# Batch 3's softmax denominators from a sum made on GpSimd, and an earlier place for one group of batch 2's query transpositions

## The chip, the cores and the metric

The kernel runs on one core of a Trainium2 chip. The metric is the device time of one execution in microseconds; the time before is the median of three runs, 233.81 us (233.22 to 233.97).

## The reference

The computation is an attention over 32 memory slots followed by a gated feed-forward layer. For each of 8 batches and 8 heads, with 576 positions and head width 64:

```python
a = softmax(phi, axis=positions)                  # 576 x 32, normalized over the positions
k_m = einsum('bhsm,bhsd->bhmd', a, k)             # 32 x 64
v_m = einsum('bhsm,bhsd->bhmd', a, v)
attn = softmax(q @ k_m^T / sqrt(64), axis=slots)  # 576 x 32
x = attn @ v_m                                    # heads side by side: 4608 x 512
out = (silu(x @ w_gate) * (x @ w_val)) @ w_out    # 512 -> 1536 -> 512
```

The first softmax needs, for each head and slot, a denominator: the sum of exp(phi) over the 576 positions. It is applied to the two sums over positions, k_m and v_m, once they are there.

## The kernel before

**Tiling.** Work goes batch by batch. Positions lie nine to a partition (JK = 9), and a head takes 64 partitions, so two heads (NG = 2 groups) fill the 128 partitions and there are four pairs of them. v_m is multiplied into w_gate and w_val first (`u_round`, L460), which gives the matrices t_U; the attention weights t_A are then the moving operand of the gate and value products (`gv_half`, L515). ScalarE takes silu of the gate (L532), VectorE multiplies it with the value (L538) into t_h. One batch has 24 such gate and value slots. The output product t_h times w_out is a two by two block product with seven instead of eight block products: its operands are sums and differences of blocks, t_S of t_h (L603 and L560, on GpSimd or VectorE) and t_T of w_out (`weight_sums`, L562, on VectorE).

**Output products.** `products` (L689) returns them as 42 small units in a fixed order: `first` (units 0 to 5 into bank p_os, 6 to 11 into p_oa), `five` (12 to 17, bank p_oc), `six` (18 to 23, p_os again), `three` (24 to 29, p_oc again), `seven` and `four`. A unit is two matrix products of 128x256 (L727), one for each half of 256 positions. Units 0 and 1 of a product use chunk 0 of the hidden width, 2 and 3 chunk 1, 4 and 5 chunk 2. After a product's last unit a copy on ScalarE (`keep`, L752, tiles t_p and t_q) or an add on VectorE (L757) reads the bank, and a bank used again waits for that.

**Order.** The order on every engine is the order in which the code is written out (L62). Items of a batch are Python closures, run by hand in lists (`run`) or put among each other by a numeric place (`spread`). An engine does its own instructions in order; where one needs a result of another engine it waits, and what stands behind it on that engine waits too. TensorE's weight loads (LDWEIGHTS) go ahead of the product that is running.

**Banks.** The eight PSUM banks are handed out from a list, the longest free first (`bank`, `done`, L75 to L84). A bank's next user waits for the last reader of the user before.

**Batch 2's start (L999 to L1024).** TensorE runs batch 0's remaining output products and, among them, batch 2's attention: k and v sums over positions (`kv_sum`, L222, tiles p_kv, one bank for each group), their normalization on VectorE (`kv_norm`, L268, four operations at L266 into t_bkv), their transposition on TensorE (`kv_T`, L278: three products at L288 into p_T, copied to t_kT by VectorE, L289), and the transposition of the queries in three groups of six (`q_T`, L377: products at L383 into p_q, copied to t_qT by ScalarE, L337). Then the scores follow (`scores`, L392: products at L396, exponentials at L407). VectorE makes the weight differences t_T meanwhile (L560). A copy of one element on GpSimd, `wait_for` (L642, tile t_mark, L645), holds GpSimd until a given tile is there; here it waits for the last of the t_T. After it GpSimd makes eight block sums of batch 1 and issues batch 4's four loads (`loads`, q, phi, k, v; L108, L94, L99, L103).

**Denominators (`kv_denominators`, L239).** exp(phi) lies in t_ephi as nine tiles of 128x128 (a position in nine, times four head pairs with 32 slots). Without further work TensorE multiplies each of the nine with `ones2`, 128x2, and adds them up in PSUM: nine weight loads and nine products two columns wide (L258). Where a batch is in `esums`, GpSimd has added the nine tiles first (`phi_sum`, L205: a mark that waits for the batch before's t_A, four adds at L212, a cast to bfloat16 at L218 and the remainder at L219), and TensorE has two products, with the sum's high and low part (tile t_ehl). Before the change batches 4, 6 and 7 are in `esums`; 2, 3 and 5 are not.

**`kv_items` (L292).** For a batch in `esums` the denominators come behind the k and v sums and a further round of products (`behind`), in a p_kv bank. For one that is not, they come first, in a bank of their own, p_S (`own`). The k and v sums of batch b + 1 are put at place 6 of the 24 slots of batch b.

Of the kernel before, what the change touches and what calls it, by code (L numbers as in the profile page):

```python
# [14 lines left out]
def kernel(  # L15
# [59 lines left out]
    def bank(shape, dtype, name):  # L75
        tag = free.pop(0)
        t = ps.tile(shape, dtype, tag=tag, name=name)
        held[id(t)] = tag, t
        return t

    def done(*tiles):

        for t in tiles:
            free.append(held.pop(id(t))[0])  # L84
# [29 lines left out]
    def load_qT(b):  # L114

        qTs[b] = att.tile([128, NS, 128], BF16, tag="qT", name="t_qT")
        nc.sync.dma_start_transpose(out=qTs[b], in_=qs[b])
# [52 lines left out]
    def phi_exp(b):  # L170
        t = att.tile([128, JK, NP, M], BF16, tag="ephi", name="t_ephi")
        nc.scalar.activation(
            out=t.rearrange("p j i m -> p i j m"),
            in_=phis.pop(b).rearrange("p i (j m) -> p i j m", m=M),
            func=AF.Exp,
        )
        ephis[b] = t
# [25 lines left out]
    esums = {}  # L203
# [18 lines left out]
    def kv_sum(b, p, parts):  # L222


        w0, w1 = parts[0], parts[-1] + 1
        n = (w1 - w0) * D
        for j in range(JK):
            for i in range(NP):
                for g in range(NG):
                    nc.tensor.matmul(  # L230
                        p[g][32 * i:32 * i + 32, 0:n],
                        lhsT=phi_of(b, g, j, i),
                        rhs=kvs[b][64 * g:64 * g + 64, w0:w1, i, j * D:(j + 1) * D],
                        start=(j == 0),
                        stop=(j == JK - 1),
                        tile_position=(64 * g, 32 * i),
                    )

    def kv_denominators(b, p):  # L239

        if b in masked:
            for g in range(NG):
                for j in range(JK):
                    nc.tensor.matmul(
                        p[:, g:g + 1],
                        lhsT=masked[b][:, j, g].rearrange("p i m -> p (i m)"),
                        rhs=ones1,
                        start=(j == 0),
                        stop=(j == JK - 1),
                    )  # L250
            return
        if b in esums:
            hl = esums.pop(b)
            terms = [hl[:, t] for t in range(2)]
        else:
            terms = [ephis[b][:, j].rearrange("p i m -> p (i m)") for j in range(JK)]
        for n, x in enumerate(terms):
            nc.tensor.matmul(p, lhsT=x, rhs=ones2, start=(n == 0), stop=(n == len(terms) - 1))  # L258

    def kv_reciprocal(b, p):  # L260
        r = att.tile([128, NG], FP32, tag="rS", name="t_rS")
        nc.vector.reciprocal(out=r, in_=p)
        rSs[b] = r
# [4 lines left out]
    def kv_norm(b, p):  # L268

        t = att.tile([128, 3, 128], BF16, tag="bkv", name="t_bkv")  # L270
        for g in range(NG):
            x = p[g][:, 0:D].rearrange("p (a d) -> p a d", a=1).to_broadcast([128, 2, D])
            scaled_copy(t[:, g].rearrange("p (a d) -> p a d", a=2), x, rSs[b][:, g:g + 1])
            scaled_copy(t[:, 2, D * g:D * g + D], p[g][:, D:2 * D], rSs[b][:, g:g + 1])
            done(p[g])
        bkvs[b] = t

    def kv_T(b):  # L278


        kTs[b] = att.tile([128, 3, 128], BF16, tag="kT", name="t_kT")
        t = bkvs.pop(b)
        if b > 3:
            nc.sync.dma_start_transpose(out=kTs[b], in_=t.rearrange("p n x -> p (n x)"))
            return
        p = bank([128, 3, 128], BF16, "p_T")
        for n in (2, 0, 1):
            nc.tensor.transpose(p[:, n], t[:, n], ident)  # L288
        nc.vector.tensor_copy(out=kTs[b], in_=p)  # L289
        done(p)  # L290

    def kv_items(b, beside=None):  # L292


        def run_sums():
            o = 2 * D
            behind = b in esums
            own = beside and not behind
            if own:
                d = bank([128, NG], FP32, "p_S")  # L300
                kv_denominators(b, d)
                kv_reciprocal(b, d)
                done(d)
            p = [bank([128, CH], FP32, f"p_kv{g}") for g in range(NG)]
            if not (own or behind):
                kv_denominators(b, p[0][:, o:o + NG])
            kv_sum(b, p, (0, 1))
            if behind:
                beside()
                kv_denominators(b, p[0][:, o:o + NG])  # L310
            if not own:
                kv_reciprocal(b, p[0][:, o:o + NG])
            kv_norm(b, p)
            if beside and not behind:
                beside()

        return [run_sums, lambda: kv_T(b)]
# [530 lines left out]
    def run(items):  # L848
        for x in items:
            x()  # L850
# [10 lines left out]
    def exp_tables():  # L861
        nc.scalar.preload_act_table_set("natural_log_exp_and_others")
# [127 lines left out]
    def run_late():  # L990
        run(late)
        late.clear()
# [3 lines left out]
    for b in range(2, B):  # L996
        last = b + 1 == B
        exp_tables()
        if b == 2:  # L999
            load_qT(3)  # L1000
            phi_exp(2)
            (zero, ops0), (one, ops1) = products(0, ("c11",)), products(1, ("p1", "c11"))
            kv, q2 = kv_items(2), q_items(2, "aaa")
            run(zero[:6])
            sums = {n: f for n, f in zip(((1, 1), (0, 2), (1, 2)), late)}
            late.clear()
            sums[0, 2]()
            weight_sums(0)
            weight_sums(1)
            run(zero[6:12] + one[:6] + kv[:1] + q2[:2])  # L1010
            weight_sums(2, (0, 1))
            run(zero[12:16] + zero[18:22] + kv[1:] + q2[2:] + zero[16:18] + zero[22:24])
            weight_sums(2, (2, 3))
            ops0["c11"]()
            ops1["p1"]()
            wait_for(Ts[2][0:1, 3, 0, 0:1])
            for part in ((0, 1), (3,), (2,)):
                for c in (1, 2):
                    sums[1, c](part)
            loads(4)  # L1020
            backlog = one[6:12] + zero[36:] + one[12:36]
            ops = ops1
        else:
            run(take(6))  # L1024
        for g in range(NG):
            scores(b, g)
        if b > 2:
            ops["p1"]()
            u_values(b)
        else:  # L1030
            run(zero[24:36] + take(6))
        run(take(6))
        z_inv_v(b, 0)
        ops["c11"]()
        run(take(6))
        if not last:
            phi_exp(b + 1)
        z_inv_v(b, 1)
        if b > 2:
            norm(b, 0)  # L1040
            norm(b, 1)
        run(take(6))
        run_late()
        if b == 4:
            wait_for(atts[4, 1][0:1, 0, 0:1])
            quad_sums(0)
        nc.scalar.preload_act_table_set("silu_and_others")
        run(take(6))
        if b == 2:
            norm(2, 0)  # L1050
        run(take(6))
        if b == 2:
            norm(2, 1)
            u_three(2)
            run(one[36:])
        g = gv_slots(b)
        quad = []
        if b == 4:
            quad = products(b, (), 0)[0]
        if last:  # L1060
            rest, rest_ops = products(b, (), 1)
            backlog += rest[:12]
        beside = 0 if last else 2 if quad else min(4, len(backlog))
        outs = [lambda: run(take(1)) for _ in range(len(backlog) - beside)]
        streams = [(g, 0, 24), (quad[:12], 0, 3), (quad[12:], 12, 18.5)]
        streams += [(outs, 4, 7 if quad else 24)]
        if b == 2:
            streams += [([lambda: u_values(2)], 2.5, 3)]
        if last:
            streams += [([u_item(b, 2)], 5, 6)]  # L1070
        if not last:
            if b > 2:
                load_qT(b + 1)
            if b > 2 and b != 4:
                phi_sum(b + 1)
            streams += [
                (kv_items(b + 1, lambda: (u_item(b, 2, "aava")(), run(take(2)))), KV, KV + 4),
                ([lambda: (u_three(b + 1), run(take(2)))], 19, 20),
            ]
        spread(*streams)  # L1080
        flush_mul()
        units, ops = products(b, ("p1", "c11"))
        backlog += units
# [34 lines left out]
```

## Time and profile before

| | |
|---|---|
| median of three runs | 233.81 us (233.22 to 233.97) |
| profiled execution, span from first to last instruction | 231.4 us; its time with what lies around the span is not listed |
| median less span | 2.4 us |
| TensorE busy | 221.6 us, 96% |
| VectorE, ScalarE, GpSimd busy | 185.1, 171.7, 140.8 us |
| batch 2's transpositions and scores | 59.1 to 63.6 us |
| batch 3's denominators, p_S | at 79.98 us |

In the profile PE is TensorE's products, PEld its weight loads, DVE VectorE, ACT ScalarE, POOL GpSimd, SP SyncE. A line of a timeline has the start in us from the span's start, the duration of what is merged in it, the engine, the line in the code, the operation, the tile written and those read, the shape and the count; in brackets stands the idle time before it and what ended it. Products are pipelined: each lasts longer than the step from one to the next. The ends of products are modelled.

### The profile page before, as it was taken

The page shows a single profiled execution, that of the slowest core. Times are in us where ns is not written, and L with a number is a line of the kernel's source. Part 1 is how long each engine was busy: PE and PEld are TensorE (multiplying, and loading weights), DVE is VectorE, ACT ScalarE, POOL GpSimd, SP SyncE. Part 2 cuts the span into 40 slices and gives each one's busy share as a digit, 9 for nine tenths or more (in the row PEclk, how much of TensorE's full clock was granted, in tenths as well). Part 3 has the DMA queues.
Part 4 walks back from the last instruction along what each step waited for, and adds up shares of the span by engine and source line. Part 5 has one row for each costly group of instructions (what it writes and reads, how often), then busy time and mean ns, then how long its engine had stood idle before and what let it go on. Part 6 is the DMA issues. An engine that isn't in the chain of part 4 may idle for free.

```text
span 231.4 us, 7210 instructions
## 1 busy us (share of the span) xinstructions
PE 221.6 (96%) x2825; PEld 169.8 (73%) x2825; DVE 185.1 (80%) x423; ACT 171.7 (74%) x365; POOL 140.8 (61%) x190
## 2 busy tenths in 40 slices
PE   6987799999999999999999999999999999999993
PEld 2544476778887777878788787887788778878882
DVE  4245789999966799989997668998999899977732
ACT  2777898988447989968896658978898789677310
POOL 8422427998199049765977689464845394039291
PEclk9999999999999999999999999999999999999998
DMA  6999999999996992999299946994014502202125
GB/s 214 210 211 206 199 207 207 221 245 268 205 225 175 256 256 49 223 204 184 71 223 191 226 134 115 252 236 89 28 65 114 104 0 95 91 10 84 31 85 160
DMA packets 36674, 36.84 MB, mean 159 GB/s; under 512 B 14624, under 2 KB 31008, under 8 KB 36640
## 3 DMA queue, kind: packets, MB, share of 16 engines
q0 software_dynamic: 16272, 22.42, 52.5%
q1 hardware_dynamic: 19600, 13.18, 22.9%
q10 hardware_dynamic: 768, 0.79, 1.1%
q8 instruction: 22, 0.36, 0.6%
q14 instruction: 12, 0.10, 0.1%
HBM read 42.47 MB, written 9.44 MB: 224 GB/s over the span
## 4 chain that ended last, share of the span: by engine, by line
PE 86%; DMA 9%; POOL 2%; ACT 1%; issue 0%; DVE 0%; POOLq 0%
PE p_g L515 21%; PE p_os L727 21%; PE p_v L515 20%; PE p_oc L727 10%; DMA W<-in_moe_w_val_dram 9%; PE p_oa L727 5%; PE p_u L472 5%; PE p_kv L230 2%; PE p_g L396 1%; POOL t_kv L99 1%; POOL t_kv L103 1%; PE p_q L383 0%; POOL t_q L108 0%; ACT t_qT L337 0%; POOL W L138 0%
## 5 line engine op out<-in xcount | busy, mean ns | idle before, releaser
L538 DVE TENSOR_TENSOR t_h<-t_sg,p_v 128x288 bf16<-128x288 bf16 x192 | 81.8, 451 | 14.1 <-PE p_v L515 7.0
L515 PEld LDWEIGHTS <-t_U 128*128 128x128 bf16 x768 | 73.9, 98 | 21.2 <-issue 3.5
L532 ACT ACTIVATE t_sg<-p_g 128x288 bf16<-128x288 f32 x192 | 73.3, 424 | 17.1 <-PE p_g L515 11.4
L515 PE MATMUL p_g<-t_A,t_U 128*128 128x288 bf16 x384 | 77.0, 286 | 0.0
L515 PE MATMUL p_v<-t_A,t_U 128*128 128x288 bf16 x384 | 77.0, 286 | 0.0
L727 PEld LDWEIGHTS <-t_S 128*128 128x128 bf16 x384 | 37.5, 98 | 4.5 <-issue 0.2
L603 POOL TENSOR_TENSOR t_S<-t_h 128x512 bf16<-128x512 bf16 x17 | 19.7, 1157 | 32.7 <-DVE t_h L538 31.2
L727 PEld LDWEIGHTS <-t_h 128*128 128x128 bf16 x288 | 27.1, 98 | 8.6 <-issue 5.0
L492 ACT CAST t_U<-p_u 128x512 bf16<-128x512 f32 x51 | 27.0, 605 | 6.6 <-PE p_u L472 6.6
L727 PE MATMUL p_os<-t_T,t_S 128*128 128x256 bf16 x192 | 23.7, 273 | 0.0
L560 POOL TENSOR_TENSOR t_S<-t_S,t_h 128x512 bf16<-128x512 bf16 x17 | 19.6, 1156 | 1.3
L560 POOL TENSOR_TENSOR t_S<-t_h 128x512 bf16<-128x512 bf16 x16 | 18.4, 1152 | 0.0
L560 POOL TENSOR_TENSOR t_S<-t_h,t_S 128x512 bf16<-128x512 bf16 x16 | 18.4, 1152 | 0.0
L472 PE MATMUL p_u<-W,t_kT 64*32 64x512 bf16 (+1 forms) x416 | 15.3, 363 | 1.2 <-DMA W<-in_moe_w_gate_dram 0.6
L496 DVE CAST t_U<-p_u 128x512 bf16<-128x512 f32 x21 | 13.6, 683 | 1.9 <-PE p_u L472 1.9
L727 PE MATMUL p_os<-t_T,t_h 128*128 128x256 bf16 x96 | 14.8, 273 | 0.0
L875 PE MATMUL p_warm<-bones 128*128 128x512 bf16 x44 | 12.5, 421 | 1.7 <-DVE bones L897 1.7
L452 DVE TENSOR_TENSOR t_A<-t_E,t_lz 128x576 bf16<-128x576 bf16 x16 | 11.4, 740 | 0.7 <-ACT t_lz L428 0.7
L727 PE MATMUL p_oc<-t_T,t_S 128*128 128x256 bf16 x96 | 11.9, 273 | 0.0
L727 PE MATMUL p_oa<-WO,t_h 128*128 128x256 bf16 x96 | 11.8, 273 | 0.0
L727 PE MATMUL p_oc<-WO,t_S 128*128 128x256 bf16 x96 | 11.8, 272 | 0.1
L727 PE MATMUL p_os<-WO,t_h 128*128 128x256 bf16 x96 | 11.8, 273 | 0.0
(107 smaller groups left out, 308.3 us busy)
## 6 DMA issues: line engine op xcount, KB each, us to landing
out_dram<-t_o SPq DMA_DIRECT2D x11, 512.0 KB, 3.0
t_kv<-in_k_dram POOLq DMA_DIRECT2D x8, 576.0 KB, 10.5
t_q<-in_q_dram POOLq DMA_DIRECT2D x8, 576.0 KB, 8.4
t_kv<-in_v_dram POOLq DMA_DIRECT2D x8, 576.0 KB, 14.7
t_phi<-in_phi_dram POOLq DMA_DIRECT2D x6, 576.0 KB, 8.1
out_dram<-t_o SPq DMA_DIRECT2D x10, 256.0 KB, 4.5
WO<-in_moe_w_out_dram POOLq DMA_DIRECT2D x3, 512.0 KB, 19.2
W<-in_moe_w_gate_dram POOLq DMA_DIRECT2D x2, 512.0 KB, 16.5
```

The lines of the kernel that those rows point to most:

```text
L230: nc.tensor.matmul(p[g][32 * i:32 * i + 32, 0:n], lhsT=phi_of(b, g, j, i), rhs=kvs[b][64 * g:64 * g + 64, w0:w1, i, j * D:(j + 1) * D], st ...
L452: nc.vector.tensor_tensor(out=a, in0=es.pop((b, g)), in1=lzs.pop((b, g)), op=ALU.mult)
L472: nc.tensor.matmul(p[g][32 * i:32 * i + 32, o:o + n], lhsT=kTs[b][64 * g:64 * g + 64, 2, 32 * i:32 * i + 32], rhs=w_part(w, c, i, g, halve ...
L492: nc.scalar.copy(out=t, in_=p)
L496: nc.vector.tensor_copy(out=t, in_=p)
L515: nc.tensor.matmul(p[:, 0:HALF], lhsT=Us[b, c, g][:, o // 2, which, 128 * (o % 2):128 * (o % 2 + 1)], rhs=atts[b, g][:, r], start=(g == 0) ...
L532: nc.scalar.activation(out=sg, in_=gate[:, 0:HALF], func=AF.Silu)
L538: nc.vector.tensor_tensor(out=dst, in0=sg, in1=val[:, 0:HALF], op=ALU.mult)
L560: eng.tensor_tensor(out=out, in0=x, in1=y, op=ALU.subtract)
L603: eng.tensor_tensor(out=t[:, 0], in0=A21, in1=A22, op=ALU.add)
L727: nc.tensor.matmul(mine[home][:, u], lhsT=lhs(c, m, u), rhs=rhs(c, m), start=fresh and u == 0, stop=(k == 5), skip_group_check=u == 1 or n ...
L875: nc.tensor.matmul(p[:, 0:128 * a], lhsT=bones, rhs=x.to_broadcast([128, a, 128]) if a > 1 else bones, start=True, stop=True,)
```

## The change

Three lines change. The first two belong together: batch 3's exponentials are summed by GpSimd as well (`phi_sum(3)` is called in batch 2's main stretch, ahead of its slots), and its denominators stay ahead of the k and v sums in a bank of their own, now as two products instead of nine. The third moves the third group of batch 2's query transpositions ahead of the first eight products of `six` and of the transposition of t_bkv.

```diff
         def run_sums():
             o = 2 * D
-            behind = b in esums
+            behind = b in esums and b != 3
             own = beside and not behind
...
             weight_sums(2, (0, 1))
-            run(zero[12:16] + zero[18:22] + kv[1:] + q2[2:] + zero[16:18] + zero[22:24])
+            run(zero[12:16] + q2[2:] + zero[18:22] + kv[1:] + zero[16:18] + zero[22:24])
             weight_sums(2, (2, 3))
...
             if b > 2:
                 load_qT(b + 1)
-            if b > 2 and b != 4:
+            if b != 4:
                 phi_sum(b + 1)
```

On GpSimd seven instructions come in between batch 4's loads and batch 2's first block sum: the mark, four adds, a cast and a subtraction. On TensorE seven weight loads and seven products go, six products with their loads move, and the banks of p_T and p_q are exchanged. VectorE and ScalarE keep their instructions and their order.

## Prediction

> **What bounds the kernel now.** I read the page first, then the chain of work that ended last, then the timeline of each engine around the two places that change.
>
> ```profile
> PE 221.6 (96%) x2825; PEld 169.8 (73%) x2825; DVE 185.1 (80%) x423; ACT 171.7 (74%) x365; POOL 140.8 (61%) x190
> PEclk9999999999999999999999999999999999999998
> PE 86%; DMA 9%; POOL 2%; ACT 1%; issue 0%; DVE 0%; POOLq 0%
> ```
>
> TensorE is busy in 96% of the span, at the full granted clock in every slice, and is 86% of the chain. In the chain's time order every step after 63.59 us is TensorE until the last store's copy at 227.64. So a time that TensorE saves after about 60 us should reach the end. Time saved elsewhere counts only where TensorE waits for it. I therefore look for TensorE's waits.
>
> The first place is batch 2's start. TensorE's timeline and ScalarE's:
>
> ```profile
> 59.80 1.04 PE L727 MATMUL p_oc<-t_T,t_S 128*128 128x256 bf16 x8
> 60.68 1.04 PE L727 MATMUL p_os<-t_T,t_S 128*128 128x256 bf16 x8
> 61.55 0.33 PE L288 MATMUL p_T<-ident,t_bkv 128*128 128x128 bf16 x3
> 61.72 0.50 PE L383 MATMUL p_q<-ident,t_q 128*128 128x128 bf16 x6
> 62.05 0.60 PE L727 MATMUL p_oc<-t_T,t_S 128*128 128x256 bf16 x4
> 62.49 0.60 PE L727 MATMUL p_os<-t_T,t_S 128*128 128x256 bf16 x4
> 63.10 0.28 PE L396 MATMUL p_g<-t_qT,t_kT 64*32 64x288 bf16 x1
> ...
> 63.59 0.38 PE L727 MATMUL p_oc<-WO,t_S 128*128 128x256 bf16 x2
> ```
>
> ```profile
> 62.25 0.80 ACT L337 COPY t_qT<-p_q 128x768 bf16<-128x768 bf16 x1 [1.08 <-PE p_q L383]
> 62.95 0.59 ACT L752 COPY t_p<-p_oc 128x512 f32<-128x512 f32 x1
> ```
>
> Columns are start, duration, engine, line, operation. The third group of query transpositions is the x6 at 61.72. Its copy ends at 63.05 and the scores (L396) start 0.05 later, at 63.10. Behind it on ScalarE stands the copy of p_oc, which ends at 63.54; the product that reuses p_oc starts 0.05 later, at 63.59. Two small waits come from one late copy.
>
> The second place is batch 3's denominators and what GpSimd does before them:
>
> ```profile
> 79.73 0.41 PE L515 MATMUL p_v<-t_A,t_U 128*128 128x288 bf16 x2
> 79.98 0.37 PE L258 MATMUL p_S<-ones,t_ephi 128*128 128x2 bf16 x9
> ```
>
> ```profile
> 74.34 0.76 POOL L103 DMA_DIRECT2D t_kv<-in_v_dram  x1
> 83.84 1.15 POOL L603 TENSOR_TENSOR t_S<-t_h 128x512 bf16<-128x512 bf16 x1 [8.75 <-DVE t_h L538]
> ...
> 99.54 0.18 POOL L645 COPY t_mark<-t_A 1x1 bf16<-1x1 bf16 x1 [2.49 <-DVE t_A L452]
> ...
> 103.11 0.43 POOL L219 TENSOR_TENSOR t_ehl<-t_es,t_ehl 128x128 bf16<-128x128 f32 x1
> ```
>
> TensorE runs its nine tiny products with no gap ahead of them. GpSimd has nothing from 75.10 to 83.84. The last two lines are batch 4's own summing, the pattern that batch 3 is to get.
>
> **Part A, the third transposition group.** Nothing is added or removed; one group of six and its ScalarE copy move ahead of the eight p_os products and the three transpositions of t_bkv.
>
> *Start of the group.* Banks are handed out in turn. Batch 2's two sums p_kv0 and p_kv1 free the next two banks, and p_T took the first, p_q the second. Now p_q takes the first. In the order of the changed program its first weight load gains a wait for VectorE, which is the second of the four t_bkv operations (L266), the last reader of p_kv0. The four run from 60.17 to 61.16; in 10 ns windows two of them still overlap at 60.71 to 60.72 and one from there on, so the second ends at 60.72 at the latest. How fast TensorE follows is seen where another weight load waits for t_bkv, in batch 5:
>
> ```profile
> 130.26 0.72 DVE L266 TENSOR_SCALAR t_bkv<-p_kv,t_rS 128x64 bf16<-128x64 f32 x3
> 131.03 0.11 PEld L515 LDWEIGHTS <-t_U 128*128 128x128 bf16 x2 [0.17 <-DVE t_bkv L266]
> 131.04 0.30 PE L515 MATMUL p_v<-t_A,t_U 128*128 128x288 bf16 x1
> ```
>
> The operations end at 130.98, the load starts 0.05 later and its product with it. So the group starts at 60.72 + 0.05 = 60.77, where without the wait it would start at 60.68: **0.09 lost**. Bounds: 0 if the bank is free in time; 0.20 if the product comes a usual load-to-product step (0.11) after the load. I take 0.09, the row of the same wait.
>
> *Scores.* In batch 3 the last product before the scores starts at 91.08 + 1.47 - 0.27 = 92.28 and the scores at 92.48, 0.20 later, with nothing awaited. In batch 2 the last one starts at 62.49 + 3 x 0.109 = 62.82, so 63.02 was possible; the wait for the copy costs 0.08. After the change the copy starts when the group ends, 60.77 + 0.50 + 0.04 = 61.31 (ScalarE's two earlier copies end at 61.17), and ends at 62.11. The three t_bkv transpositions start at 60.77 + 0.33 + 0.87 = 61.97 and end at 62.30; t_kT's copy (0.36) ends at 62.70. Neither binds. Scores at 63.02 + 0.09 = 63.11.
>
> *The product behind.* The p_oc copy no longer stands behind the transposition copy. p_oc ends at 62.05 + 0.60 + 0.09 = 62.74. From such a product to such a copy took 0.09 at 70.39 (the product ended at 70.30), so the copy runs 62.83 to 63.42 and lets the product go at 63.47. The scores themselves hold it too: its first weight load stood 0.37 after the scores' start (63.47 against 63.10), which gives 63.11 + 0.37 = 63.48. The later is 63.48, against 63.59: **0.11 gained** in all. Bounds from the two ends of the bank wait: 0.20 gained (scores 63.02, product 63.39), and 0 (scores 63.22, product 63.59).
>
> *What comes later.* t_kT's copy starts at 62.34 instead of 61.92, and VectorE's two differences behind it (L560), then GpSimd's mark at 63.01 and all it has queued move by up to 0.43: eight sums to 72.33, four loads to 75.10, now 75.53. The sum that TensorE needs soonest after its end is the last: done at 72.33 + 0.43 = 72.76, its first reader is the ninth product of the p_os row at 72.76, 72.76 + 8 x 0.109 - 0.11 = 73.52. Covered by 0.76. VectorE's add of p_oa ends at 63.55 + 0.43 = 63.98 and that bank is refilled at 66.21. The first reader of what those loads bring is batch 4's exponential at 96.39, so 0.43 there costs nothing. If these covers went, a late sum would cost TensorE at most the 0.43.
>
> **Part B, the summing.** *Removed:* seven of nine load and product pairs. The row above has nine products of 163 ns in 0.37: (0.37 - 0.163) / 8 = 0.026 from one to the next. 7 x 0.026 = **0.18 gained**. The nearest other row, batch 4's two products (104.53 to the next at 104.59), shows 0.03 each, 0.21; I keep 0.18. Below: 0, if the p_kv sums behind waited for their banks instead; the VectorE products that free those are done by 80.01.
>
> *Added:* on GpSimd one mark and six operations. Batch 4's take 99.54 to 103.54, **4.00**; the same at 152.15 and 175.74. They start when GpSimd is free (75.53) and when batch 2's second t_A is there. That ended at 74.90 + 0.75 = 75.65, follows TensorE's products and so comes 0.11 sooner: 75.54. From t_A's end to the mark took 0.12 in batch 3 (99.42 to 99.54). Mark at 75.66, sum done at 79.66. TensorE wants it for the second weight load, at 79.98 - 0.11 = 79.87. With 0.05 for the release there is **0.16 to spare**. So the wait is new and costs nothing, but barely. Behind it on TensorE's queue stands everything: the k and v sums, the gate and value products, hence ScalarE and VectorE. Behind the mark on GpSimd stands the sum at 83.84, which has 4 us left.
>
> VectorE beside GpSimd: its L538 products average 451 ns from 76.5 to 80.6 with GpSimd idle, and 455 ns from 100.0 to 103.6 beside the same six operations. No loss there.
>
> The Trainium skill speaks against the place: "GPSIMD Engine Reference", section "Engine selection", sends an add on a tile to VectorE, GpSimd being about 2 times slower with two inputs. In this trace GpSimd is idle for 8.75 us where the 4.00 falls, while VectorE is busy 2.56 of the 4.00 us from 76 to 80. The page's 2.6 cycles an element at 1.2 GHz (section "Elementwise — side-by-side cycle accounting") make an estimate of 2.5 us for the five two-input operations, against 3.7 in the rows; by it the spare time would be over 1 us, and the sum the same.
>
> **Sum.** -0.11 - 0.18 = -0.29 us. The page gives the profiled execution's span, 231.4, which becomes 231.1. The median of the three runs is 233.81, 2.4 above the span; I take the difference over: **233.5**. The runs shown spread over 0.75 us, and about 0.3% (0.7 us) is what a measurement of this kernel can tell from no change.
>
> **Rivals.**
> 1. *The sum comes late, and the kernel is slower.* Place: TensorE's second weight load for p_S. If GpSimd ends later than 79.82, all of TensorE stands. For: only 0.16 is spare, and mark, sums and loads queue ahead. Against: all three summings took 4.00 to within 0.01. Each us late beyond 0.16 costs a us; from 0.45 late on it outweighs the gain. If one operation of VectorE's length there (0.68) were waited for at each of two operations, 1.36 late: -0.29 + 1.36 - 0.16 = +0.9, 234.7.
> 2. *The bank is free in time:* Part A gives 0.20, all 0.38, 233.4. The windows of t_bkv speak against it.
> 3. *The gain is lost on the way*, because a later stage is set by VectorE (no gap from 83.67 to 88.6) and TensorE arrives there only to wait: 233.8. For: VectorE is as full as TensorE there. Against: no TensorE gap is seen in it.
> 4. *Part A loses instead:* wait 0.20, gain 0, so only 0.18: 233.6.
>
> **Chances.** Forecast 0.48; rival 2 0.12; rival 3 0.16; rival 4 0.08; rival 1 0.16. No case by itself gains 0.7 us; from the spread of the runs and what I can't see I give faster by over 0.3% 0.12. Slower by over 0.3% needs rival 1 over 1 us late, or scatter: 0.13. Within 0.3%: 0.75. Range: the forecast less the runs' lower half-spread, 0.6, is 232.9; rival 1's smaller half and the upper scatter reach 234.3.
>
> **What would show it.** The group's x6 at about 60.77 and not 60.68; scores at about 63.1; the p_oc product at about 63.48; GpSimd's mark at about 75.7 and t_ehl done at about 79.7; p_S as x2 at about 79.87 with the k sums 0.12 behind. Wrong if PEld L258 shows a wait for GpSimd, if t_h grows beyond 460 ns beside the sums, or if the gain at 80 us is gone at 100.

## The result, and the profile after

The changed kernel takes **232.81 us** (median of 11 runs, 232.73 to 233.14). In the same job the kernel before took 233.41 us (11 runs, 233.14 to 233.97). The ratio is 0.9978, with a 95% interval of 0.9971 to 0.9986: 0.51 us less, between 0.33 and 0.68; the two medians lie 0.60 apart. Forecast were 233.5 us in a range of 232.9 to 234.3, and 0.29 us less. So the direction is right and the size of the change is inside the 0.3% that got the chance of 0.75. The time lies 0.09 us below the range.

The changed page first, section by section as the prediction read it: busy times, the granted clock, the chain.

```profile
PE 221.2 (96%) x2818; PEld 169.4 (73%) x2818; DVE 185.0 (80%) x423; ACT 171.7 (74%) x365; POOL 144.2 (62%) x197
PEclk9999999999999999999999999999999999999998
PE 87%; DMA 9%; POOL 2%; issue 0%; DVE 0%; POOLq 0%
```

TensorE has seven products and seven loads fewer and 0.4 us less busy time; GpSimd has seven instructions and 3.4 us more. TensorE is now 87% of the chain, and ScalarE's 1% is gone from it.

**Part A.** TensorE's timeline of the changed kernel at batch 2's start, then ScalarE's and VectorE's:

```profile
59.67 1.04 PE L727 MATMUL p_oc<-t_T,t_S 128*128 128x256 bf16 x8
60.61 0.51 PE L383 MATMUL p_q<-ident,t_q 128*128 128x128 bf16 x6
60.95 1.04 PE L727 MATMUL p_os<-t_T,t_S 128*128 128x256 bf16 x8
61.83 0.33 PE L288 MATMUL p_T<-ident,t_bkv 128*128 128x128 bf16 x3
...
62.96 0.29 PE L396 MATMUL p_g<-t_qT,t_kT 64*32 64x288 bf16 x1
...
63.33 0.94 PE L727 MATMUL p_oc<-WO,t_S 128*128 128x256 bf16 x7
```

```profile
62.63 0.58 ACT L752 COPY t_p<-p_oc 128x512 f32<-128x512 f32 x1 [0.68 <-PE p_oc L727]
```

```profile
62.19 0.36 DVE L289 COPY t_kT<-p_T 128x384 bf16<-128x384 bf16 x1 [0.40 <-PE p_T L288]
```

The x6 now stands ahead of the eight p_os products. ScalarE waits 0.68 us for p_oc and has nothing in front of that copy. The group's first weight load waited for VectorE:

```profile
60.60 0.34 PEld L383 LDWEIGHTS <-t_q 128*128 128x128 bf16 x6 [0.18 <-DVE t_bkv L266]
```

The first p_oc product of this trace stands at 59.67 where the one before stood at 59.80: 0.13 us come from the stretch ahead, whose code is the same, and are not the change's. They have to be taken off before the forecast is compared.

**Part B.** TensorE and GpSimd at batch 3's denominators, and VectorE's main group from the page:

```profile
79.49 0.41 PE L515 MATMUL p_v<-t_A,t_U 128*128 128x288 bf16 x2
79.73 0.19 PE L258 MATMUL p_S<-ones,t_ehl 128*128 128x2 bf16 x2
79.86 0.80 PE L230 MATMUL p_kv<-t_kv,t_ephi 64*32 64x128 bf16 x72
```

```profile
74.61 0.75 POOL L103 DMA_DIRECT2D t_kv<-in_v_dram  x1
75.47 0.18 POOL L645 COPY t_mark<-t_A 1x1 bf16<-1x1 bf16 x1
75.61 1.14 POOL L212 TENSOR_TENSOR t_es<-t_ephi 128x512 f32<-128x512 bf16 x1
...
79.03 0.43 POOL L219 TENSOR_TENSOR t_ehl<-t_es,t_ehl 128x128 bf16<-128x128 f32 x1
83.41 1.15 POOL L603 TENSOR_TENSOR t_S<-t_h 128x512 bf16<-128x512 bf16 x1 [3.96 <-DVE t_h L538]
```

```profile
L538 DVE TENSOR_TENSOR t_h<-t_sg,p_v 128x288 bf16<-128x288 bf16 x192 | 81.7, 451 | 14.2 <-PE p_v L515 7.0
```

Two products stand where nine stood, with no idle time ahead of them in the record, and the k sums follow 0.12 us later. The six operations fill 75.61 to 79.46, and GpSimd still waits 3.96 us afterwards. VectorE's products average 451 ns.

**Where the 0.49 us between the two spans lies.** I cut TensorE's timeline at four products that both kernels have: the first output product (A), the p_oc product behind batch 2's scores (B), the first k sum of batch 3 (C) and that of batch 4 (D).

| us | before | after | difference | forecast |
|---|---|---|---|---|
| start to A | 54.160 | 54.029 | -0.131 | 0 |
| A to B (Part A) | 9.431 | 9.302 | **-0.129** | -0.11 |
| B to C (Part B) | 16.684 | 16.524 | **-0.160** | -0.18 |
| C to D | 22.636 | 22.637 | +0.001 | 0 |
| D to TensorE's last product | 124.415 | 124.424 | +0.009 | 0 |
| last product to the end | 4.111 | 4.035 | -0.076 | 0 |
| span | 231.437 | 230.951 | -0.486 | -0.29 |

The two changed steps sum to -0.289 us. The other 0.20 lies in stretches whose code is the same. The question for the experiments is whether the 0.20 is part of the change's effect, and how the comparison of many runs comes to 0.5.

### The profile page after: what moved, and what is told of

Same layout as the page of the kernel before. It is cut to its first block, busy times and chain, and to the rows that moved or that the text cites. A ratio compares the mean times of both kernels' runs of the same rounds, so it can differ in the third digit from the quotient of the medians.

```text
span 231.0 us, 7204 instructions
## 1 busy us (share of the span) xinstructions
PE 221.2 (96%) x2818; PEld 169.4 (73%) x2818; DVE 185.0 (80%) x423; ACT 171.7 (74%) x365; POOL 144.2 (62%) x197
## 4 chain that ended last, share of the span: by engine, by line
PE 87%; DMA 9%; POOL 2%; issue 0%; DVE 0%; POOLq 0%
PE p_os L727 21%; PE p_g L515 21%; PE p_v L515 20%; PE p_oc L727 10%; DMA W<-in_moe_w_val_dram 9%; PE p_oa L727 5%; PE p_u L472 5%; PE p_kv L230 2%; PE p_g L396 1%; POOL t_kv L99 1%; POOL t_kv L103 1%; PE p_q L383 1%; POOL t_q L108 0%; POOL W L138 0%; DVE t_q L339 0%
```

## The experiments

**Theory 1:** the program gains what its two steps show, 0.29 us, and no more; the remainder lies in runs of the kernel before that lose time elsewhere, and in the base that the prediction started from. **Rivals:** one part alone brings it all; the bank wait or GpSimd's sum costs something that the steps hide; the place of the instructions changes the early stretch. "Before" is timed again in each job: 233.30, 233.47, 233.43 and 233.52 us in the four jobs below (22 to 35 runs each).

| kernel | us (runs) | ratio, 95% | A to B | B to C |
|---|---|---|---|---|
| e1_same | 233.75 (233.26 to 234.47) | 1.0014 [1.0002, 1.0026] | 9.431 | 16.682 |
| e2_group | 233.29 (232.94 to 233.74) | 0.9995 [0.9985, 1.0005] | 9.298 | 16.695 |
| e3_sum | 232.97 (232.82 to 233.13) | 0.9981 [0.9972, 0.9991] | 9.469 | 16.508 |
| e4_bank | 232.79 (232.67 to 233.02) | 0.9974 [0.9965, 0.9983] | 9.229 | 16.521 |
| e5_late | 233.83 (233.69 to 234.01) | 1.0017 [1.0008, 1.0026] | 9.304 | 17.513 |
| e6_late_small | 233.33 (one run) | | 9.291 | 16.823 |
| e7_behind | 233.94 (233.85 to 234.09) | 1.0021 [1.0011, 1.0032] | 9.300 | 16.493 |
| e8_warm | 233.36 (233.15 to 233.56) | 0.9989 [0.9975, 1.0004] | 9.430 | 16.683 |
| e11_before_warm | 233.36 (233.11 to 234.09) | 0.9998 [0.9987, 1.0009] | 9.432 | 16.684 |
| e9_after_warm | 233.00 (232.88 to 233.88) | 0.9980 [0.9968, 0.9991] | 9.310 | 16.520 |
| e10_bank_warm | 232.85 (232.69 to 233.38) | 0.9975 [0.9963, 0.9987] | 9.228 | 16.522 |
| e12_after_again | 232.88 (232.77 to 233.01) | 0.9976 [0.9967, 0.9986] | 9.308 | 16.522 |
| e13_seven_back | 233.16 (232.97 to 233.88) | 0.9992 [0.9981, 1.0004] | 9.297 | 16.699 |
| e14_sum_unused | 233.34 (233.04 to 233.94) | 0.9992 [0.9982, 1.0001] | 9.433 | 16.684 |
| e15_look | 233.51 (one run) | | 9.598 | 16.684 |
| e16_look | 233.26 (one run) | | 9.430 | 16.683 |

### The same code again: e1_same

The kernel before with a blank line at its end.

> The kernel before, unchanged, timed against itself. It tells how much of the measured difference (ratio 0.9978, about 0.5 us, where the two traces show 0.29 us at the two changed places and 0.13 us in the first 26 us, which are the same code) is scatter. Theory 1 (the change is worth what the trace shows at its two places, 0.29 us; the rest is scatter of the early stretch): ratio 1.000 with a half interval of about 0.001, and a trace whose TensorE times before 59 us differ from the first trace by around 0.1 us. Theory 2 (the change is worth the whole 0.5 us): ratio 1.000 with an interval so narrow, under 0.0005, that 0.29 and 0.51 us are clearly apart, and early times that repeat to within 0.03 us.

The same instructions came out 0.14% longer than the kernel before, with an interval that leaves out 1. The profiled execution took 234.11 us. From A on its steps are those of before to within 0.01 us; it is 0.93 us late at A, 0.23 of it already at the products that waited for v. TensorE's wait for v in this trace, then the stretch after it (start and end, us, busy time of PE, PEld, DVE, ACT, POOL, granted clock, DMA share, GB/s):

```profile
21.27 0.76 PE L325 MATMUL p_mT<-t_mphi,t_kv 128*64 128x64 bf16 x36 [1.64 <-DMA t_kv<-in_v_dram]
```

```profile
22.00:26.00 4.00, 3.88 (x41) 1.85 (x41) 1.65 (x5) 3.63 (x7) 1.05 (x3) 0.62 1.41 197
```

The same two views of the kernel before:

```profile
21.04 0.76 PE L325 MATMUL p_mT<-t_mphi,t_kv 128*64 128x64 bf16 x36 [0.62 <-DMA t_kv<-in_v_dram]
```

```profile
22.00:26.00 4.00, 3.24 (x56) 1.56 (x54) 2.38 (x9) 3.89 (x8) 0.77 (x2) 1.00 1.41 197
```

TensorE stood 1.64 us instead of 0.62, and the granted clock from 22 to 26 us was 0.62 instead of 1.00 (in windows of half a microsecond it is 0.50 from 23 to 26 us). A difference of 0.1% between kernels of this program is thus within what its scatter makes; what is compared to hundredths below are the steps of the traces.

### One part at a time: e2_group and e3_sum

```diff
-            run(zero[12:16] + zero[18:22] + kv[1:] + q2[2:] + zero[16:18] + zero[22:24])
+            run(zero[12:16] + q2[2:] + zero[18:22] + kv[1:] + zero[16:18] + zero[22:24])
```

> Only the third transposition group is moved; batch 3 keeps its nine denominator products. Theory 1: the p_oc product behind the scores comes 0.13 us sooner against its own early stretch (0.11 was forecast), nothing further is gained, ratio about 0.9995. Theory 2: the move is worth more than the place shows, about 0.3 us, ratio 0.9986.

e3_sum has the other two lines of the change alone:

```diff
-            behind = b in esums
+            behind = b in esums and b != 3
...
-            if b > 2 and b != 4:
+            if b != 4:
```

> Only batch 3's sum is moved to GpSimd; the transposition group stays where it was. Theory 1: the k and v sums of batch 3 come 0.16 to 0.18 us sooner, t_ehl is done 0.2 us or more before TensorE wants it, ratio about 0.9993. Theory 2: the sum is worth about 0.3 us, ratio 0.9986, by something outside its place. Rival of a late sum: p_S stands in a wait for GpSimd and the ratio is 1.000 or above.

The steps separate: Part A alone takes 0.133 us off A to B and leaves B to C as it was to 0.011, Part B alone takes 0.176 off B to C (its A to B has 0.04 more, from a wait for q's load at 59.2). Neither hides the other. The medians do not follow: Part A's is 0.01 under the kernel before, Part B's 0.33, and e3_sum's interval leaves out the 0.9993 that Theory 1 gave for it. The trace of e2_group holds 0.20 us more than before near 135 us, in a stretch that the change doesn't touch.

### The bank wait taken away: e4_bank

The changed kernel with the list of free banks turned by hand, so that the third group's p_q gets a bank that is long free:

```diff
-            run(zero[12:16] + q2[2:] + zero[18:22] + kv[1:] + zero[16:18] + zero[22:24])
+            run(zero[12:16])
+            free.insert(0, free.pop(2))
+            run(q2[2:] + zero[18:22] + kv[1:] + zero[16:18] + zero[22:24])
```

> The changed kernel, with the third transposition group given the bank that the first group has left, so that it no longer waits for VectorE's reading of p_kv0. If the bank wait costs what the changed trace shows (the group starts 0.06 us after the last p_oc product's step, 0.09 was forecast), the group starts 0.06 us sooner, and so do the scores and the p_oc product behind them: 0.06 us, ratio 0.9975 where the change alone has 0.9978. If that wait costs nothing because the copy of p_oc holds the product anyway, the product stays where it is.

TensorE's timeline of e4_bank:

```profile
59.64 1.04 PE L727 MATMUL p_oc<-t_T,t_S 128*128 128x256 bf16 x8
60.52 0.50 PE L383 MATMUL p_q<-ident,t_q 128*128 128x128 bf16 x6
...
63.23 0.61 PE L727 MATMUL p_oc<-WO,t_S 128*128 128x256 bf16 x4
```

The group starts 0.88 us after the p_oc row instead of 0.94, and A to B is shorter by 0.073 than in the changed kernel, 0.202 than in the one before. That is the price of the bank wait (forecast 0.09) and the 0.20 of rival 2. At 232.79 us this is the fastest kernel here, though 0.02 from the changed one in the medians.

### The sum made late: e5_late and e6_late_small

e5_late makes the sum's first 128x512 add twice (the second time over the first, so the sum is the same):

```diff
         add(t, e[:, 0:4], e[:, 4:8])
+        if b == 3:
+            add(t, e[:, 0:4], e[:, 4:8])
```

> The changed kernel with GpSimd's first and longest add of batch 3's sum (128x512, 1.15 us) made twice; the result is the same. In the changed trace t_ehl is done 0.27 us before the second weight load that reads it, 0.22 with the release. If that is the whole cover, TensorE waits 1.15 - 0.22 = 0.9 us at the denominators, nothing behind gives it back, and the kernel is about 0.6 us slower than before (ratio 1.002) and 0.9 slower than the changed kernel. If work behind has slack that swallows the wait, the loss is smaller than 0.9 by that slack.

e6_late_small adds one dead 128x128 add instead:

```diff
+        if b == 3:
+            add(t[:, 3], t[:, 0], t[:, 1])
```

> The changed kernel with one more small add (128x128, 0.43 us and some 0.1 to the next) in batch 3's sum; its output is not used. With a cover of 0.22 us TensorE waits about 0.3 us and the k and v sums of batch 3 start 0.3 us later against the output product behind the scores than in the changed kernel (16.52 us behind it there). With a cover of more than 0.55 us they start no later.

TensorE and GpSimd of e5_late (its L260 is the L258 of before):

```profile
80.20 0.18 PE L260 MATMUL p_S<-ones,t_ehl 128*128 128x2 bf16 x1 [0.34 <-ACT t_sg L534]
80.71 0.18 PE L260 MATMUL p_S<-ones,t_ehl 128*128 128x2 bf16 x1 [0.33 <-POOL t_ehl L221]
80.81 0.80 PE L232 MATMUL p_kv<-t_kv,t_ephi 64*32 64x128 bf16 x72
```

```profile
79.86 0.29 POOL L220 CAST t_ehl<-t_es 128x128 bf16<-128x128 f32 x1
80.23 0.42 POOL L221 TENSOR_TENSOR t_ehl<-t_es,t_ehl 128x128 bf16<-128x128 f32 x1
```

The last operation ends at 80.65, the second product starts 0.06 later, and the k sums stand 0.99 us later than in the changed kernel. The first line names ScalarE, but the load of that product came from the cast that ended at 80.15. C to D is 22.637 as in the changed kernel: nothing gives the loss back. The extra add took 1.2 us, so 0.2 of it was covered. With the small add B to C grows by 0.30 for an operation of about 0.5: again 0.2 of cover. So rival 1 is a real mechanism, each microsecond beyond the cover costing a microsecond as forecast, and the changed kernel stands 0.2 us away from it.

### Denominators behind the sums: e7_behind

The changed kernel without `and b != 3`: batch 3's two products go behind the k and v sums, as in batches 4, 6 and 7.

```diff
-            behind = b in esums and b != 3
+            behind = b in esums
```

> The changed kernel with batch 3's denominators behind the k and v sums and the round of products, as in batches 4, 6 and 7, instead of ahead of them. The same TensorE work in another order: k and v sums 0.1 us sooner, the end the same, ratio 0.9978 to 0.9975. The sum then has about 1.4 us more to spare. If the normalization on VectorE, which now waits for the denominators, holds the bank that a gate or value product needs, up to 0.2 us is lost, ratio 0.9985.

It is 0.21% slower than the kernel before, and my expectation was wrong. TensorE and VectorE of e7_behind:

```profile
83.28 0.34 PE L288 MATMUL p_T<-ident,t_bkv 128*128 128x128 bf16 x3 [0.55 <-DVE t_bkv L266]
```

```profile
81.43 0.69 DVE L496 CAST t_U<-p_u 128x512 bf16<-128x512 f32 x1 [0.67 <-PE p_u L472]
82.04 0.16 DVE L262 RECIPROCAL t_rS<-p_kv 128x2 f32<-128x2 f32 x1
82.23 0.99 DVE L266 TENSOR_SCALAR t_bkv<-p_kv,t_rS 128x128 bf16<-128x128 f32 x4
```

The same reciprocal of the changed kernel, and its transposition on TensorE:

```profile
80.42 0.16 DVE L262 RECIPROCAL t_rS<-p_S 128x2 f32<-128x2 f32 x1
```

```profile
82.02 0.33 PE L288 MATMUL p_T<-ident,t_bkv 128*128 128x128 bf16 x3
```

B to C is even 0.03 shorter, but the reciprocal comes 1.62 us later (0.27 of it from the stretch ahead of A), behind a cast of VectorE, and TensorE waits for t_bkv: C to D is 23.672 instead of 22.637. Of these 1.03 us, 0.71 lie between the transposition and the product before it (82.45 to 83.28, where the changed kernel has 81.90 to 82.02). Another 0.24 lie ahead of the pair of products at 82.32, which waited for a t_U from ScalarE. The gain depends on the denominators being there early, so a bank of their own is part of Part B.

### Dummy products at the start: e8_warm, e11_before_warm, e9_after_warm, e10_bank_warm

`warm(12)`, three products of 128x512 (twelve times 128 columns; the expectations call them twelve products) whose result nobody reads, behind the second group of scores, where e1_same had idled. e8_warm and e11_before_warm are the kernel before with it, e9_after_warm the changed kernel, e10_bank_warm e4_bank.

```diff
+    warm(12)
```

> The kernel before with 12 more dummy products (about 0.7 us) in the early stretch, after batch 1's scores, where TensorE waits for v. In the repeat of the kernel before TensorE idled 1.6 us there and the granted clock then was 0.62 from 22 to 26 us, and the run was 0.9 us longer; in the first trace it idled 0.9 us and the clock was 1.00. If the slow runs of the kernel before (233.6 to 234.5 us) come from this clock, they go: the runs lie within 0.4 us and the median near 233.2. If they come from elsewhere, the spread of 1.2 us stays.

> The kernel before with the 12 early dummy products that kept the granted clock at 1.00 in the run before (all runs 233.15 to 233.56 there). It is the base that the next two are compared with: median near 233.3 again.

> The changed kernel with the same 12 early dummy products. Theory 1 (the change is worth the 0.29 us that the traces show at its two places, the rest of the measured 0.5 us being scatter of the early stretch in the kernel before): its median lies 0.2 to 0.4 us under that of the kernel before with the dummy products. Theory 2 (the change is worth 0.5 us): 0.45 to 0.6 us under it.

> The changed kernel with the bank of the first group for the third group, and the 12 early dummy products. In the trace with that bank the product behind the scores came 0.20 us sooner than in the kernel before, against 0.13 with the change alone. So 0.36 us under the kernel before with the dummy products, and 0.07 under the changed kernel with them: the fastest of these if the early stretch does not hide it.

e8_warm's runs lie within 0.41 us as expected, but its median is 233.36 and not 233.2. (In the first trace the wait for v is 0.62 us by the row above, not 0.9 as its expectation has it.) With the same start the changed kernel is 0.36 us under the one before and e10_bank_warm 0.51. The first is what Theory 1 gives, 0.29 from the steps and 0.07 of scatter; the second is 0.15 above its steps' 0.36. Of the 23 runs of the kernel before with `warm(12)` one is over 233.6 us. Of the 59 runs without it in the same two jobs 21 are. But single long runs come back in e9_after_warm too (233.88, the profiled one), late at A by 0.62 and with 0.47 near 135 us, so the start alone is not the whole scatter.

### TensorE's stream or GpSimd's: e12_after_again, e13_seven_back, e14_sum_unused

e12_after_again is the changed kernel once more. e13_seven_back is the changed kernel with seven narrow products ahead of p_S's two, which the two overwrite:

```diff
+        if b == 3:
+            for j in range(7):
+                y = ephis[b][:, j].rearrange("p i m -> p (i m)")
+                nc.tensor.matmul(p, lhsT=y, rhs=ones2, start=True, stop=True)
```

e14_sum_unused is the kernel before with batch 3's sum made by GpSimd and not used:

```diff
-            if b > 2 and b != 4:
+            if b != 4:
                 phi_sum(b + 1)
+            if b == 2:
+                esums.pop(3)
```

> The changed kernel again, built and loaded anew. If a load of its own has an offset of 0.1 to 0.15 us, as the two timings of the kernel before suggest, its ratio lies anywhere from 0.997 to 0.999, and its first output product anywhere from 54.0 to 55.1 us, while the steps from there to the end repeat to 0.01 us but for a hole near 135 us.

> The changed kernel with seven further products two columns wide ahead of batch 3's two (the tiles of the exponentials again, their result overwritten), so that TensorE has as many instructions as in the kernel before while GpSimd still makes the sum. The price of the seven: the k and v sums of batch 3 start 0.16 to 0.18 us later behind the output product (16.52 us in the changed trace), unless the cover of the sum takes up some of it. The slow tail of the kernel before (33 of 104 runs over 233.6 us, of the changed kernel 0 of 23): if it hangs on TensorE's instruction stream, it returns (3 or 4 of 12 runs over 233.6); if it hangs on GpSimd's, it stays away and the runs lie within 0.4 us.

> The kernel before with batch 3's sum made on GpSimd but not used: TensorE keeps its nine products. It costs nothing if GpSimd was idle there: the steps from the first output product on are those of the kernel before (9.43, 16.68, 22.64 us) to 0.01 us. The slow tail: if it hangs on GpSimd's instructions it is gone, runs within 0.4 us and a median near 233.2; if on TensorE's, 3 or 4 of 12 runs are over 233.6.

The changed kernel repeats to 0.01 us in its steps. The seven products cost 0.175 us, 25 ns each. The sum that nobody uses leaves A to B, B to C and C to D of the kernel before as they were, to 2 ns: GpSimd's 4 us there cost TensorE nothing. The Trainium skill ("GPSIMD Engine Reference", section "Engine selection") sends adds on a tile to VectorE. No run here put these adds there; what this run shows is that on an idle GpSimd they cost TensorE nothing.

### Two more traces of the kernel before: e15_look and e16_look

> The kernel before, one more trace. If it is a run over 233.6 us, the theory of the early clock wants a granted clock under 1.00 between 18 and 30 us and the first output product over 54.4 us, with the later steps unchanged; the theory of a later hole wants the loss after it.

> The kernel before, one more trace, for the same question: where a run over 233.6 us loses its time.

TensorE's loads and products of e15_look, then the same products of the trace before:

```profile
59.06 0.67 PEld L383 LDWEIGHTS <-t_q 128*128 128x128 bf16 x12 [0.24 <-DMA t_q<-in_q_dram]
```

```profile
134.79 0.41 PE L515 MATMUL p_v<-t_A,t_U 128*128 128x288 bf16 x2
135.43 0.71 PE L727 MATMUL p_oc<-t_T,t_Q 128*128 128x256 bf16 x5 [0.23 <-issue]
```

```profile
134.85 0.41 PE L515 MATMUL p_v<-t_A,t_U 128*128 128x288 bf16 x2
135.09 0.71 PE L727 MATMUL p_oc<-t_T,t_Q 128*128 128x256 bf16 x5
```

This run lost 0.17 us at the wait for q and 0.39 near 135 us, where TensorE waited for nothing that the profile shows ("issue"). In e16_look it is 0.22 there. In the first trace before, in after, e1_same, e3_sum, e4_bank and e12_after_again it is at most 0.02. The clock was 1.00 in both places. Neither is a run over 233.6 us, so they do not answer where such a run loses its time.

## Why the prediction was wrong

**The step that failed is the last line of the sum, the base:** "The median of the three runs is 233.81, 2.4 above the span; I take the difference over". What lies around the span is 1.77 to 1.81 us in all 17 profiled executions whose time is on record (e1_same 234.11 with a span of 232.34, after 232.73 with 230.95). The profiled execution of before, span 231.44, therefore took about 231.44 + 1.78 = 233.22, which is the lowest of the three listed runs; the median of three was another execution. Over the 126 runs of the kernel before that were timed beside the others (the three listed among them) the median is 233.40, a tenth are under 233.15 and a third (42) over 233.6; two of the three listed ones were of that third. So the base was 0.59 too high for the execution whose span was read, and 0.41 for the median of many runs. From 233.22 the working gives 232.93, 0.12 above the result; from 233.40 it gives 233.11, 0.30 above; from 233.81 it gave 233.52, 0.71 above. The range failed with it: its lower end, the forecast less 0.6, comes to the lowest of the three runs less the gain, and the lowest of the 126 runs, 233.03, is 0.19 below that one.

**Part A held.** On the early offset of -0.13 the forecast places were 60.64 for the group, 62.98 for the scores and 63.35 for the product; measured 60.61, 62.96 and 63.33. The wait for VectorE's second t_bkv cost 0.06 to 0.07 (forecast 0.09), as e4_bank shows. Rival 2 did not happen and rival 4 neither. GpSimd's mark came 0.40 late net of the offset (forecast 0.43) and nobody waited for what it delayed.

**Part B held.** Forecast 0.18, measured 0.160, and 0.175 when the seven were put back. The mark stood at 75.47 (75.53 by the forecast with the offset), the sum was done at 79.46, and the cover forecast at 0.16 is about 0.2 by e5_late and e6_late_small. Rival 1 did not happen; rival 3 fell with C to D unchanged. The prediction's 3.7 us for GpSimd's five two-input operations takes in the mark: from 99.68 to 103.54 less the cast of 0.29 they are 3.6, and no term of the sum hangs on it. The prediction bounded the row of p_S but left unsaid why the denominators stay ahead of the sums; e7_behind shows a cost of 1.03 us if they do not.

**Why many runs show 0.51 and not 0.29** is shown in part. The lowest run of 126 before is 233.03, the lowest of 23 of the changed kernel 232.73: 0.30 apart, close to the steps' sum. But the lowest quarter ends at 233.22 and at 232.81, 0.41 apart, and the medians are 0.52 apart. The kernel before has a third of its runs over 233.6 and the changed kernel none of 23 over 233.2; without the runs over 233.6 the medians are still 0.40 apart. So the long runs explain about half of what exceeds 0.29. The other 0.1 us lies neither in the two steps nor in the long runs, and that the change is worth "no more" than its steps isn't shown for the runs. Only one traced run of the kernel before is over 233.6, e1_same, and it lost its time ahead of A. Smaller losses are seen at the wait for q at 59.1 (e15_look) and near 135 us (e15_look, e16_look). None of these is code that the change touches.

**What stays open** is why the changed kernel is spared. The long runs are absent in after, e12_after_again, e3_sum and e4_bank (46 runs, spreads of at most 0.41 us), and e5_late and e7_behind spread as little (18 runs, at most 0.32). All six have seven products and loads fewer on TensorE. Long runs are present in before, e1_same, e2_group, e13_seven_back (2 of 12 over 233.6) and e14_sum_unused (1 of 12), which have as many as before. That speaks for TensorE's stream and against GpSimd's, but 12 runs with one or two long ones don't settle it, and the kernels with `warm(12)`, which have three products more, have few long runs as well. A late load of instructions does not explain the loss near 135 us. On the queue that loads them (22 packets of 16 KB) the packet nearest to the place starts at 132.7 to 133.5 us in e2_group, e15_look, e16_look and e9_after_warm. But it starts at 132.6 to 133.4 also in e1_same, e3_sum, e4_bank, e5_late and e12_after_again, which lost nothing there, and at 132.2 in e8_warm, which lost 0.25.

## What to carry to other kernels

Tie a forecast to the profiled execution's own time, its span plus what lies around a span, and not to a median of three runs; when the two stand apart, the median belongs to other executions. A result is needed at the weight load, not at the product: moving this reduction to an idle engine was worth what TensorE dropped, because the chain of six small operations ended before that load, and in e5_late every microsecond beyond the cover was paid in full. Compare kernels that differ by 0.1% step by step between common products, since the same code timed twice differed by 0.14% here.

## What the runs showed of the hardware that was not expected

- **The granted clock fell once, behind a short idle.** In e1_same the granted clock was 0.62 over 4 us after TensorE had stood for 1.64 us among busy stretches; with 0.62 us of waiting (before) and with 1.35 (e4_bank) it stayed at 1.00. The page "TensorE: Matmul & The Clock Gate" of the Trainium skill, section "Part 1: The HAM clock gate", speaks of an idle window of about 3.4 us before the clock drops; this row shows a drop after less than half of that. The length of the idle alone does not decide it: in e14_sum_unused TensorE stood for 1.81 us before 18.89 us, and the clock stayed at 1.00. What does is open.
- **A product whose load waits follows its releaser by 0.06 us** (80.65 to 80.71 in e5_late). Such a wait can cost less than its length: in the changed kernel the load at 60.60 had waited 0.18 us, and e4_bank shows a cost of 0.06 to 0.07, since in the same rows a load stands 0.11 ahead of its product.
- **TensorE can lose 0.2 to 0.5 us in a place where it waits for no other engine** (e15_look, e16_look, e2_group, e8_warm, e9_after_warm near 135 us), in some executions of the same code and not in others.
